# Chunked linear attention and a squared-ReLU layer: a fourth pair of blocks in the paired path, single-value scalars, a folded column sum, two banks lent, and a new order

## The chip, the cores and the metric

One core of a Trainium2 chip runs the whole kernel. The metric is device time in microseconds (us), the median of several executions. The engines are PE (matrix multiply), DVE (vector), ACT (scalar), POOL (GpSimd) and SP, which in this kernel only issues DMAs.

## The reference, cut to what matters

```python
# q, k, v, alpha: [4 batches, 8 heads, 768 steps, 48]
for t in range(S):
    state = alpha[:, :, t, :, None] * state + k[:, :, t] (x) v[:, :, t]     # 48 x 48 a head
    y[:, :, t] = q[:, :, t] @ state
x = y as [3072 tokens, 384]
h = x @ w_in                      # 384 x 2048
g = s * relu(h) ** 2 + b          # s and b are one number each
out = g @ w_out                   # 2048 x 384
```

Since b is one number, `b * (column sums of w_out)` is a row that is added to every row of the output; the kernel works it out once (`bias_w`) and multiplies by s at the very end.

## The kernel before, in words

The 3072 tokens are 24 blocks of 128, six to a batch. For a block the kernel takes logarithms of alpha (`ln2`), sums them along time by a matmul with a triangle of ones (`cum2` or `cumA`), exponentiates both ways (`eb`, `ei`, and `el` for the block's end), scales q and k (`mul1`, `mul2`), transposes them, forms the masked 128 x 128 scores (`A`, `mk`), the state's increment (`KV`, then `t1` on DVE and `sn` on POOL) and the output (`y`, copied out by `ye`). The layer then takes blocks two at a time, as 12 groups: `mm1.g.u.w` is one eighth of a group's first matmul into bank `h_ps[w]`, `re` on ACT is the ReLU into one of two buffers, `sq` on DVE the square, `mm2.n.jq` a quarter of block n's second matmul, `oe` the end on DVE, `st` the store.

Blocks come in two layouts. The first `NPAIR` pairs of blocks are loaded a pair at a time (`ld2`, 384 KB: each partition holds an even and an odd time step, so that each contiguous run in memory is 2 x 48 x 4 = 384 bytes), and use `cum2`, `mul2`, `KV2`, `A2`, `mk2`, `y2`. The later blocks are loaded singly (`ld1`, 192 KB in runs of 192 bytes) and use the forms with a 1; only alpha is always loaded by pairs. Pairs 0 to 2 are transposed on PE (`T2`) and copied out (`Tc2`); from block 6 on `T1` transposes by a DMA from one on-chip buffer to another, issued by SP. Each of q, k, v and alpha has four pair-sized input buffers, so a load waits until the pair four before it has been read.

The weights come in eight blocks of 768 KB: `ld_i.0` to `ld_i.3` for w_in and `ld_o.0` to `ld_o.3` for w_out, into staging buffers. `ci` and `co` cast them to bf16, `cp` adds the two halves of a w_out block, `ca` adds two of these partial sums; `bm` multiplies a tile of ones by b, `bmm` sums over the partitions on PE in fp32, `bc` copies the result out, and the first `oe` waits for it. `ld_bs` loads b and s. `F.n` are n filler matmuls on zeros.

No scheduler runs: the order of everything is the list `PROGRAM`, written out by hand item by item. Each engine, and SP as the queue of DMAs, executes its own items in the list's order, and an item that waits holds all behind it on the same engine. Names carry block, pair or group numbers, and the engine where there is a choice.

Of the kernel before, what the change touches and what calls it, by code (L numbers as in the profile page):

```python
# [8 lines left out]
FP32 = mybir.dt.float32  # L9
# [6 lines left out]
NPAIR = 3  # L16
# [21 lines left out]
ye.1.ACT c_V2 ci.0.ACT ld2.q.2 F.5.h1 KV2.1 mk2.1.1.0 mm1.0.3.1 t1.2 ld2.k.2 mk2.1.0 re.0.3.1.0.ACT
mm1.0.1.0 sn.2.POOL ln2.2 mm1.0.0.1 t1.3 re.0.1.0.1.ACT sq.0.3.0.DVE F.3.o1 y2.1 ci.2.ACT ld_o.2
sq.0.1.1.DVE sn.3.POOL mm1.0.2.0 vc2.2.0.POOL ld1.v.6 re.0.0.1.0.ACT ye.2.DVE vc2.2.1.POOL ye.3.DVE  # L40
cum2.2.1 re.0.2.0.1.ACT sq.0.0.0.DVE ld_o.0 cum2.2.0 eb2.2.1 blk2.2 sq.0.2.1.DVE mm1.1.0.1 ei2.2.1
mul2.q.2.1.DVE eb2.2.0 mm1.1.2.0 ld_i.3 mul2.k.2.1.DVE ei2.2.0 mul2.q.2.0.DVE el2.2 re.1.0.1.0.ACT
mul2.k.2.0.DVE T2.2.0.c re.1.2.0.1.ACT sq.1.0.0.DVE T2.2.1.y Tc2.2.0.c.ACT mm1.1.1.1 ld_o.1 cp.2.DVE
mm1.0.4.0 re.1.1.1.0.ACT Tc2.2.1.y.DVE ld2.a.3 vc1.6.POOL sq.1.2.1.DVE A2.2.0.a sq.1.1.0.DVE mm1.1.3.1
re.0.4.0.1.ACT mk2.2.0 co.2.ACT KV2.2 mm1.0.5.0 co.0.POOL ld1.k.6 t1.4 A2.2.1.a re.1.3.1.0.ACT
sq.0.4.1.DVE mm2.0.0 sn.4.POOL mk2.2.1 re.0.5.0.1.ACT ld1.k.7 mm1.1.4.1 ci.3.ACT ld_bs sq.0.5.1.DVE y2.2
sq.1.3.0.DVE cp.0.DVE re.1.4.1.1.ACT mm1.1.5.0 co.1.DVE ye.5.ACT ye.4.ACT ld1.q.6 cp.1.DVE mm1.2.6.1
ln2.3 ld1.q.7 sq.1.4.1.DVE re.1.5.0.0.ACT cumA.3 ca.0.1.DVE ld_o.3 re.2.6.1.1.ACT blk2.3 mm1.0.6.0 ei1.6
sq.2.6.1.DVE ld1.v.7 sq.1.5.0.DVE eb1.6 mm1.2.4.1 bm re.0.6.0.1.ACT mul1.k.6.DVE mm2.0.1 re.2.4.1.0.ACT
mul1.q.6.DVE mm1.2.3.0 ei1.7 sq.2.4.0.DVE T1.6 eb1.7 sq.0.6.1.DVE mm1.0.7.1 re.2.3.0.0.ACT mul1.k.7.DVE  # L50
KV1.6 mul1.q.7.DVE mm1.2.5.0 re.0.7.1.1.ACT sq.2.3.0.DVE T1.7 el2.3 mm1.2.0.1 sq.0.7.1.DVE
re.2.5.0.0.ACT cp.3.DVE mm1.1.7.0 re.2.0.1.1.ACT ld2.a.4 co.3.ACT mm1.2.1.1 ld1.k.9 sq.2.5.0.DVE
ca.2.3.DVE ld1.k.8 mm2.0.2 ld1.q.8 re.2.1.1.0.ACT t1.6 vc1.7.POOL mm2.0.3 ca.0.2.POOL KV1.7 A1.6 t1.7
mm1.1.6.1 mk1.6 bmm Ay.7 bc ln2.4 ld1.v.9 oe.0 mm2.1.0 ye.6.ACT sq.2.1.0.DVE ld1.q.9 mm2.1.1
sq.2.0.1.DVE re.1.6.1.0.ACT mk1.7 cumA.4 ld2.a.5 blk2.4 mm1.2.7.1 ei1.8 eb1.8 ld1.v.8 mm2.1.2
mul1.k.8.DVE ei1.9 mul1.q.8.DVE mm2.1.3 eb1.9 mul1.k.9.DVE re.1.7.0.1.ACT T1.8 mm2.2.0 vc1.9.POOL oe.1
el2.4 sn.7.POOL mm1.2.2.0 st.0 mm2.2.1 sq.1.7.1.DVE mul1.q.9.DVE mm2.3.0 ln2.5 sq.1.6.0.DVE T1.9 mm2.2.2
re.2.7.1.1.ACT vc1.8.POOL mm2.3.1 st.1 KV1.8 mm2.2.3 t1.8 ld1.v.11 mm2.3.2 ld1.q.10 oe.2 sn.8.POOL Ay.8
ld1.k.11 sq.2.7.1.DVE ld1.k.10 mm2.4.0 ye.7.ACT mk1.8 re.2.2.0.0.ACT KV1.9 mm2.3.3 sq.2.2.0.DVE
mm1.3.3.1 t1.9 mm1.3.7.0 re.3.3.1.1.ACT sn.9.POOL ld1.q.11 Ay.9 mm1.3.6.1 ld1.v.13 ye.8.ACT mk1.9  # L60
re.3.7.0.0.ACT cumA.5 ld1.v.10 blk2.5 oe.3 mm1.3.1.0 eb1.10 el2.5 ld2.a.6 mm2.4.1 eb1.11 mul1.q.10.DVE
ei1.10 mm2.4.2 ei1.11 mul1.k.10.DVE mm2.5.0 sq.3.3.1.DVE T1.10 sq.3.7.0.DVE re.3.1.0.1.ACT mm2.4.3
mul1.k.11.DVE re.3.6.1.0.ACT mul1.q.11.DVE mm2.5.1 sq.3.6.0.DVE T1.11 mm1.3.0.0 vc1.10.POOL vc1.11.POOL
mm2.5.2 re.3.0.0.0.ACT ld1.v.12 KV1.10 ln2.6 mm1.3.2.1 sq.3.0.0.DVE ld1.q.12 oe.4 mm1.3.5.0 st.2
re.3.2.1.0.ACT t1.10 mm2.5.3 st.4 sq.3.1.1.DVE Ay.10 ld1.q.13 ld1.k.12 mm2.6.0 ye.9.ACT mk1.10
vc1.13.POOL re.3.5.0.1.ACT mm1.4.0.1 sq.3.2.0.DVE mm1.4.1.0 ld1.k.13 sq.3.5.1.DVE re.4.0.1.0.ACT
vc1.12.POOL Ay.11 re.4.1.0.1.ACT sn.10.POOL ld1.k.15 mm1.3.4.1 ye.10.ACT oe.5 cumA.6 sq.4.0.0.DVE blk2.6
sq.4.1.1.DVE mm1.4.7.0 ei1.12 ld2.a.8 re.3.4.1.0.ACT mm2.7.0 st.3 el2.6 eb1.12 sq.3.4.0.DVE mm2.7.1
re.4.7.0.1.ACT mul1.q.12.DVE mm2.6.1 mul1.k.12.DVE mm1.4.3.1 mk1.11 T1.12 mm2.6.2 re.4.3.1.0.ACT mm2.7.2
eb1.13 ld2.a.7 ei1.13 mul1.q.13.DVE mm2.7.3 sq.4.7.1.DVE mm1.4.6.0 oe.7 KV1.12 mul1.k.13.DVE mm1.4.2.1  # L70
re.4.6.0.1.ACT T1.13 mm2.6.3 sq.4.6.1.DVE sq.4.3.0.DVE re.4.2.1.1.ACT mm1.4.4.0 t1.12 ld1.k.14 mm1.4.5.1
oe.6 re.4.4.0.0.ACT ld1.v.16 Ay.12 ln2.8 ld1.q.14 ld1.q.15 mm2.8.0 ye.11.ACT mk1.12 ln2.7 mm2.9.0
sq.4.2.1.DVE KV1.13 mm1.5.6.0 t1.13 mm2.9.1 re.5.6.0.1.ACT sn.13.POOL Ay.13 ld1.v.15 sq.5.6.1.DVE
# [24 lines left out]
sq.8.3.1.DVE mk1.19 mm2.14.2 re.8.1.0.1.ACT mm2.15.2 eb1.21 sq.8.1.1.DVE mm1.8.5.1 mul1.k.21.DVE
# [23 lines left out]
def kernel(  # L122
# [130 lines left out]
    def c_ones(*_):  # L253
        nc.gpsimd.memset(ones_f, 1.0)
# [542 lines left out]
```

## Time and profile before

| | |
|---|---|
| time, 3 runs | median 188.2 us (187.43 to 188.76) |
| the profiled execution | 189.13 us, of which the span of the profile is 187.4 us |
| TensorE clock granted | 1.00 |
| busy share of the span | PE 93%, DVE 69%, ACT 57%, POOL 22% |
| DMA | 104586 packets, 34.97 MB; queue q1 77.7% of 16 engines |
| TensorE's last matmul ends | 183.9 us |

The span begins with the first instruction and ends with the last. A line such as L728 is the line of the kernel; SPq is the DMA queue of SP, and "DMA x<-y" a transfer in flight. Blocks are known in the trace by their times: `bmm` is L352, `bc` L361, `cp` and `ca` L338, `oe` L737, the scaling of k and q by pairs L422 and singly L561, `sq` L723, `mm1` L694 and `mm2` L728.

### The profile page before, as it was taken

How to read it: one execution, taken by the hardware profiler on the slowest of the kernel's cores; microseconds unless marked ns; L12 is line 12 of the kernel's file. 1: busy time of each engine (PE TensorE's matmuls, PEld its weight loads, DVE VectorE, ACT ScalarE, POOL GpSimd, SP SyncE). 2: the span in 40 equal slices, each digit the busy share in tenths (PEclk: the TensorE clock that was granted, in tenths of full speed). 3: DMA queues.
4: the chain of work that ended last, by engine and by line, in shares of the span. 5: the costliest groups of instructions: out<-in, count | busy, mean ns of one | idle time of the engine just before them, and what ended most of it. 6: DMA issues, size and time to landing. Idle time of an engine off the chain costs nothing.

```text
span 187.4 us, 5561 instructions
## 1 busy us (share of the span) xinstructions
PE 174.6 (93%) x2297; PEld 124.0 (66%) x2297; DVE 129.5 (69%) x253; ACT 106.9 (57%) x203; POOL 40.6 (22%) x78
## 2 busy tenths in 40 slices
PE   7696997888999999997999999999999999999992
PEld 6474775666566667765667677677677676777761
DVE  2475979979796776449778978588677596364341
ACT  3939996978252565654574565764762643564220
POOL 7198505101343103200111502021201301010000
PEclk9999999999999999999999999999999999999999
DMA  5999999979998799969978999989948554002013
GB/s 149 319 346 372 297 298 382 248 154 262 206 212 177 157 205 178 201 129 249 193 157 207 184 247 172 230 136 240 196 104 166 145 118 123 0 22 110 3 42 126
DMA packets 104586, 34.97 MB, mean 187 GB/s; under 512 B 97905, under 2 KB 103025, under 8 KB 104561
## 3 DMA queue, kind: packets, MB, share of 16 engines
q1 hardware_dynamic: 104560, 34.61, 77.7%
q8 instruction: 18, 0.29, 0.7%
q14 instruction: 8, 0.06, 0.1%
HBM read 25.17 MB, written 4.72 MB: 159 GB/s over the span
## 4 chain that ended last, share of the span: by engine, by line
PE 65%; SPq 20%; DMA 6%; DVE 4%; issue 2%; ACT 0%; DVEq 0%; ACTq 0%
PE o_ps L728 30%; PE h_ps L694 24%; SPq L285 8%; SPq L278 5%; PE py_ps L626 4%; SPq L301 3%; DMA k_in<-in_k_dram 3%; PE a_ps L604 3%; DMA wst<-in_moe_w_out_dram 3%; SPq L307 2%; PE ct_ps L537 2%; PE py_ps L591 1%; DVE gt L723 1%; PE ct_ps L390 1%; DVE colsum L338 1%
## 5 line engine op out<-in xcount | busy, mean ns | idle before, releaser
L704 ACT ACTIVATE r<-h_ps 128x512 bf16<-128x512 f32 x96 | 56.1, 597 | 44.4 <-PE h_ps L694 28.1
L694 PE MATMUL h_ps<-xd,w_in_bf 128*128 128x256 bf16 x576 | 74.3, 273 | 2.6 <-ACT r L704 2.2
L728 PE MATMUL o_ps<-w_out_bf,gt 128*128 128x384 bf16 x384 | 71.3, 326 | 0.0
L694 PEld LDWEIGHTS <-w_in_bf 128*128 128x128 bf16 x576 | 53.9, 98 | 14.2 <-issue 3.4
L723 DVE TENSOR_TENSOR gt<-r 128x512 bf16<-128x512 bf16 x96 | 41.9, 457 | 18.3 <-ACT r L704 17.7
L728 PEld LDWEIGHTS <-gt 128*128 128x128 bf16 x384 | 36.3, 98 | 20.2 <-issue 0.3
L672 POOL TENSOR_TENSOR s_st<-t,blast 128x384 bf16<-128x384 bf16 x16 | 14.4, 902 | 53.1 <-DVE t L662 33.3
L322 POOL CAST vp<-v_in 128x384 bf16<-128x384 f32 x21 | 11.5, 557 | 63.8 <-DMA v_in<-in_v_dram 60.9
L613 DVE TENSOR_TENSOR am<-a_ps,U 128x1024 bf16<-128x1024 f32 x18 | 22.0, 1220 | 2.5 <-PE a_ps L604 2.2
L737 DVE SCALAR_TENSOR_TENSOR o_sb<-o_ps,s_col,bias_w 128x384 f32<-128x384 f32 x24 | 14.6, 614 | 7.7 <-PE o_ps L728 5.5
L320 ACT ACTIVATE xd<-py_ps 128x384 bf16<-128x384 f32 x20 | 9.8, 490 | 12.5 <-PE py_ps L626 12.5
L561 DVE TENSOR_TENSOR qk<-k_in,binv 128x384 bf16<-128x384 f32 x18 | 10.8, 603 | 6.1 <-ACT binv L551 3.5
L662 DVE TENSOR_TENSOR t<-py_ps,s_st 64x192 bf16<-64x192 f32 x28 | 9.9, 354 | 6.6 <-PE py_ps L591 5.1
L369 ACT ACTIVATE la<-a_in 128x768 bf16<-128x768 f32 x12 | 10.1, 843 | 7.4 <-DMA a_in<-in_alpha_dram 7.3
L561 DVE TENSOR_TENSOR qk<-q_in,b_s 128x384 bf16<-128x384 f32 x18 | 10.6, 589 | 3.3 <-DMA q_in<-in_q_dram 1.9
L604 PEld LDWEIGHTS <-qkT 64*128 64x128 bf16 x144 | 4.1, 94 | 4.7 <-issue 4.7
L626 PE MATMUL py_ps<-am,vp 128*32 128x128 bf16 x288 | 7.2, 219 | 0.0
L604 PE MATMUL a_ps<-qkT 64*128 64x128 bf16 x144 | 7.2, 219 | 0.0
L759 PEld LDWEIGHTS <-zeros 128*128 128x128 bf16 x81 | 5.9, 117 | 1.4 <-DVE half L220 1.3
L320 ACT ACTIVATE w_in_bf<-wst 128x1536 bf16<-128x1536 f32 x4 | 5.9, 1482 | 0.2 <-DMA wst<-in_moe_w_in_dram 0.2
L759 PE MATMUL a_ps<-zeros 128*128 128x120 bf16 x48 | 4.4, 273 | 1.3 <-DVE half L220 1.3
L390 PEld LDWEIGHTS <-la 128*128 128x128 bf16 x96 | 3.5, 96 | 3.1 <-issue 2.5
(102 smaller groups left out, 149.9 us busy)
## 6 DMA issues: line engine op xcount, KB each, us to landing
a_in<-in_alpha_dram SPq DMA_DIRECT2D x12, 384.0 KB, 4.6
v_in<-in_v_dram SPq DMA_DIRECT2D x18, 192.0 KB, 4.3
k_in<-in_k_dram SPq DMA_DIRECT2D x18, 192.0 KB, 4.4
q_in<-in_q_dram SPq DMA_DIRECT2D x18, 192.0 KB, 4.2
out_dram<-o_sb SPq DMA_DIRECT2D x18, 192.0 KB, 2.7
wst<-in_moe_w_in_dram SPq DMA_DIRECT2D x4, 768.0 KB, 8.0
wst<-in_moe_w_out_dram SPq DMA_DIRECT2D x2, 768.0 KB, 6.0
gt<-in_moe_w_out_dram SPq DMA_DIRECT2D x2, 768.0 KB, 8.2
```

The lines of the kernel that those rows point to most:

```text
L285: nc.sync.dma_start(out=whole(ins[x], m).rearrange("a s e -> a (s e)").rearrange("a (h f) -> a h f", h=H), in_=src[x][b, :, c * C : (c + 2 ...
L320: nc.scalar.activation(out=out, in_=in_, func=AF.Copy)
L561: on(eng).tensor_tensor(out=half_of(qk, n)[:, "qk".index(x), :, 0:D], in0=half_of(ins[x], n).rearrange("a (h d) -> a h d", d=D), in1=half_ ...
L604: nc.tensor.matmul(out=a_ps[:, e, 128 * p : 128 * p + 128], lhsT=T[r, 1, p, :], rhs=T[r, 0, p, :], start=True, stop=True,)
L613: nc.vector.tensor_tensor(out=half_of(am, n).rearrange("a e p t -> a (e p) t"), in0=a_ps.rearrange("a e (p t) -> a (e p) t", t=128), in1=U ...
L626: nc.tensor.matmul(out=y_out(py_ps, x), lhsT=(st[:, p, c0 : c0 + 32] if e is None else v1[:, p, c0 + 48 * e : c0 + 48 * e + 32]), rhs=qT[: ...
L672: on(eng).tensor_tensor(out=s_sb[n % 3], in0=t1_sb[n % 2], in1=bl.unsqueeze(2).to_broadcast([128, NP, 96]), op=ALU.mult,)
L694: nc.tensor.matmul(out=h_ps[w][:, i * n : (i + 1) * n], lhsT=w_in_bf[:, kk, 128 * j : 128 * (j + 1)], rhs=xd_sb[g % 3][:, kk, 0:n], start= ...
L704: nc.scalar.activation(out=r_sb[i], in_=h_ps[w], func=AF.Relu)
L723: on(eng).tensor_tensor(out=unit_out(g, u), in0=r, in1=r, op=ALU.mult)
L728: nc.tensor.matmul(out=o_ps[n % 2][:, 0:d_model], lhsT=gt_of(n)[:, j, c0 : c0 + C], rhs=w_out_bf[:, j, :], start=(j == 0), stop=(j == NJ - 1),
L737: nc.vector.scalar_tensor_tensor(out=out_sb[n % 3], in0=o_ps[n % 2][:, 0:d_model], scalar=s_col, in1=bias_w, op0=ALU.mult, op1=ALU.add,)
```

## The change

`NPAIR` is 4, so blocks 6 and 7 take the paired path; their transposes stay with the DMA. `KV2` and `t1` of pair 0 use the two `h_ps` banks. b and s are loaded as two single numbers into row 0 of a zeroed tile, spread to all partitions by a matmul with ones (`bsm`) and copied out (`bsc`). `cf` adds the two halves of the summed column tile on DVE, and `bmm` is one matmul in place of two. The order is new throughout, and some items change engine.

```diff
-NPAIR = 3
+NPAIR = 4
 CUM_IN_H = [1]
+KV_IN_H = [0]
...
+    bs_in = sb.tile([128, 2], FP32, name="bs_in")
+    bs = sb.tile([128, 2], FP32, name="bs")
+    b_col, s_col = bs[:, 0:1], bs[:, 1:2]
...
     def c_ones(*_):
         nc.gpsimd.memset(ones_f, 1.0)
+        nc.gpsimd.memset(bs_in, 0.0)
...
     def ld_bs(*_):
-        nc.sync.dma_start(out=b_col, in_=moe_b.to_broadcast((128, 1)))
-        nc.sync.dma_start(out=s_col, in_=moe_s.to_broadcast((128, 1)))
+        nc.sync.dma_start(out=bs_in[0:1, 0:1], in_=moe_b.unsqueeze(0))
+        nc.sync.dma_start(out=bs_in[0:1, 1:2], in_=moe_s.unsqueeze(0))
...
+    def bsm(*_):
+        nc.tensor.matmul(out=o_ps[1][:, 0:2], lhsT=ones_f, rhs=bs_in, start=True, stop=True)
+
+    def bsc(*_):
+        nc.vector.tensor_copy(out=bs, in_=o_ps[1][:, 0:2])
+
+    def cf(eng="POOL"):
+        c = colsum[0]
+        add_on(eng, c[:, 0:d_model], c[:, 0:d_model], c[:, d_model : 2 * d_model])
+
     def bmm(*_):
-        for e in range(2):
-            nc.tensor.matmul(
-                out=o_ps[1][:, 0:d_model],
-                lhsT=bones,
-                rhs=colsum[0][:, d_model * e : d_model * (e + 1)],
-                start=(e == 0),
-                stop=(e == 1),
-            )
+        nc.tensor.matmul(
+            out=o_ps[1][:, 0:d_model], lhsT=bones, rhs=colsum[0][:, 0:d_model], start=True, stop=True
+        )
...
+    def kv_ps(m):
+        return h_ps if m in KV_IN_H else (py_ps, ct_ps)
```

`KV2` writes to `kv_ps(m)[c]`, and `t1` reads `kv_ps(m)[c]` for the paired blocks.

SP's list up to the loads of block 9, before and after (items of SP alone, in their order):

```
before: ld2.a.0 ld2.a.1 ld2.q.0 ld2.k.0 ld2.k.1 ld2.v.0 ld2.q.1 ld2.v.1 ld_i.1 ld_i.0 ld2.a.2 ld_i.2 ld2.v.2
        ld2.q.2 ld2.k.2 ld_o.2 ld1.v.6 ld_o.0 ld_i.3 ld_o.1 ld2.a.3 ld1.k.6 ld1.k.7 ld_bs ld1.q.6 ld1.q.7
        ld_o.3 ld1.v.7 T1.6 T1.7 ld2.a.4 ld1.k.9 ld1.k.8 ld1.q.8 ld1.v.9 ld1.q.9 ...
after:  ld2.a.0 ld2.a.1 ld2.q.0 ld2.k.0 ld2.v.0 ld2.k.1 ld2.q.1 ld_i.1 ld2.v.1 ld_i.0 ld2.a.2 ld_o.0 ld_bs
        ld2.q.2 ld2.k.2 ld2.v.2 ld_o.1 ld_i.3 ld2.v.3 ld_i.2 ld_o.3 ld2.a.3 ld_o.2 ld2.k.3 ld2.q.3 ld2.a.7
        ld2.a.4 ld2.a.6 ld1.q.12 T1.6 T1.7 ld1.v.8 ld1.q.8 ld1.k.9 ld1.k.8 ld1.v.10 ld1.q.9 ld1.v.9 ...
```

Behind the last load of blocks 6 and 7, up to and with the load of block 12's k, SP's list holds T1.6, T1.7 and: before, 3 pair loads, 17 single loads, 4 transposes and the stores of 4 blocks; after, 4 pair loads, 18 single loads, 4 transposes and the stores of 3 blocks. Shortly ahead of that load stand st.2 and st.4 before, T1.10 and T1.11 after.

DVE's list from the end of `t1.3` to the copy of `bias_w`, the same way:

```
before: sq.0.3.0 sq.0.1.1 ye.2 ye.3 sq.0.0.0 sq.0.2.1 mul2.q.2.1 mul2.k.2.1 mul2.q.2.0 mul2.k.2.0 sq.1.0.0 cp.2
        Tc2.2.1 sq.1.2.1 sq.1.1.0 mk2.2.0 t1.4 sq.0.4.1 mk2.2.1 sq.0.5.1 sq.1.3.0 cp.0 co.1 cp.1 sq.1.4.1
        ca.0.1 sq.2.6.1 sq.1.5.0 bm mul1.k.6 mul1.q.6 sq.2.4.0 sq.0.6.1 mul1.k.7 mul1.q.7 sq.2.3.0 sq.0.7.1
        cp.3 sq.2.5.0 ca.2.3 t1.6 t1.7 mk1.6 bc
after:  sq.0.1.1 co.0 sq.0.2.1 cp.0 sq.0.3.0 mul2.q.2.1 mul2.k.2.1 mul2.q.2.0 mul2.k.2.0 sq.1.0.0 sq.0.0.1 bsc
        Tc2.2.0 sq.1.1.0 cp.1 sq.1.3.1 bm mk2.2.0 t1.4 sq.1.2.0 mk2.2.1 co.1 sq.0.6.0 sq.0.7.1 cp.3 sq.1.7.0
        sq.1.6.1 co.3 sq.0.4.0 sq.1.5.1 co.2 cp.2 sq.2.3.1 sq.0.5.0 mul2.k.3.0 mul2.q.3.0 mul2.k.3.1 mul2.q.3.1
        sq.2.5.0 ca.2.3 sq.1.4.0 ca.0.2 sq.2.7.0 cf t1.6 bc
```

Items that change engine: `ci.1` from ACT to POOL; `co.0` from POOL, `co.2` and `co.3` from ACT to DVE; `ca.0.1` from DVE to POOL, `ca.0.2` from POOL to DVE; the scaling of k of pair 1 from POOL to DVE; `ye.2` and `ye.3` from DVE to ACT; the casts of v of pair 2 from POOL to ACT and one of pair 1 the other way; `Tc2.1.1` from ACT to DVE. Fillers are 100 instead of 81.

## The prediction

> **What bounds the kernel now.** I read the page first (slices, then the chain that ended last), then busy time in stretches, then DVE's instructions in order of time, and last DVE's waits.
>
> ```profile
> PE   7696997888999999997999999999999999999992
> DVE  2475979979796776449778978588677596364341
> DMA  5999999979998799969978999989948554002013
> ...
> PE 65%; SPq 20%; DMA 6%; DVE 4%; issue 2%; ACT 0%; DVEq 0%; ACTq 0%
> ```
>
> A slice is 4.7 us. From slice 11 on PE is full but for one dip (slice 19, 84 to 89 us), and the chain is PE's for 65% of the span. Ahead of that it is SP's and the DMAs' (26%). So three stretches: a front of 50 us, PE's own stretch to 183.9, and a tail of 3.5 us (a copy and a store) that the change leaves as it is. In the front, the stretches show two engines at their limit (the columns: busy us of PE, PEld, DVE, ACT, POOL, clock, DMA share, GB/s):
>
> ```profile
> 10.00:15.00 5.00, 4.04 (x104) 3.41 (x108) 4.16 (x8) 1.94 (x6) 4.71 (x9) 1.00 1.11 359
> 20.00:50.00 30.00, 26.73 (x424) 19.41 (x424) 26.31 (x50) 23.41 (x40) 8.01 (x9) 1.00 0.98 266
> 50.00:90.00 40.00, 38.90 (x479) 26.25 (x476) 28.48 (x54) 20.55 (x43) 6.95 (x10) 1.00 0.94 185
> ```
>
> The DMAs are full throughout, and DVE is busy 26.3 of 30 us between 20 and 50. What DVE waits for there and in the dip:
>
> ```profile
> 28.17 0.96 DVE L338 TENSOR_TENSOR colsum<-wst 128x768 f32<-128x768 f32 x1 [1.16 <-DMA wst<-in_moe_w_out_dram]
> 40.98 0.56 DVE L561 TENSOR_TENSOR qk<-q_in,b_s 128x384 bf16<-128x384 f32 x1 [1.20 <-DMA q_in<-in_q_dram]
> 43.99 0.96 DVE L338 TENSOR_TENSOR colsum<-wst 128x768 f32<-128x768 f32 x1 [0.17 <-DMA wst<-in_moe_w_out_dram]
> 49.99 0.56 DVE L361 COPY bias_w<-o_ps 128x384 f32<-128x384 f32 x1 [0.44 <-PE o_ps L352]
> 83.44 0.56 DVE L561 TENSOR_TENSOR qk<-k_in,binv 128x384 bf16<-128x384 f32 x1 [2.65 <-DMA k_in<-in_k_dram]
> ```
>
> The first three are late transfers, and 43.99 is the landing of the last weight block. The dip is one late load, block 12's k. I use `bmm` (L352) as the marker at which both kernels' rests are compared, since the first `oe` and all of the second matmuls behind it need it.
>
> **DMA.** At 10 to 15 us mostly pair loads and weights run, at 359 GB/s: 384 KB take 393,216 B / 359 = 1.1 us, a weight block 2.2. At 50 to 90 single loads dominate: 185 / 0.94 = 197 GB/s, so 192 KB take 1.0 us. A second row for it: alpha of pair 3 landed at 36.41 (the cast that waited for it) and block 6's q at 40.98; between them lie three single loads and the two broadcasts of b and s, 4.57 us. With 1.0 to 1.2 a single load, the broadcasts cost 1.57 to 0.97. Six single loads less, three pair loads more and no broadcasts save 6x - 3.3 + (4.57 - 3x) = 1.27 + 3x, which is 4.3 to 4.9; I take 4.6. Two single numbers I take as nothing: no row shows so small a load, but 0.0 to the 0.5 us that SP needs for any load is its bound. The Trainium skill, "DMA: Bandwidth & Descriptors", section Specifications, asks for at least 512 bytes a piece for line rate, which neither 192 nor 384 reaches; by it three pairs would cost 6.6 and the gain on loads be nil, 1.3 in all. The rows above disagree with that reading, and I go by them.
>
> What comes when: `ld_o.0` stands where `ld_i.2` stood, which landed at 21.64. Alpha of pair 3 has 14 pair loads and 7 weights up to it instead of 13, 1 single load and 7: again 36.4. Then `ld_o.2`, the last weight, 38.6 (before 43.99), and k and q of pair 3 at 39.7 and 40.8.
>
> **DVE up to the marker.** Steps from start to start in DVE's list: `sq` 0.335 (two in 0.67), `cp`, `ca`, `co` 0.87, scalings 0.48, `mk` 1.20, `t1` 0.77, `Tc2` 0.60, `ye` 0.47, `bm` 0.20. Before, from 21.60 to `bc` at 49.99: 18 x 0.335 + 7 x 0.87 + 8 x 0.48 + 3 x 1.20 + 3 x 0.77 + 0.60 + 2 x 0.47 + 0.20 = 23.6 of 28.4 us, so 4.8 of waits: 2.53 for DMAs (the lines above), 0.44 for `bmm`, 0.44 for a `KV` and 1.4 in small pieces. After, up to the end of `cf`: 19 x 0.335 + 10 x 0.87 + 8 x 0.48 + 2 x 1.20 + 0.77 + 0.60 + 0.20, half a `ca` for `cf` (0.45) and 0.2 for the two-column `bsc` (between 0.06, the shortest memset, and 0.56) = 23.5. So DVE does the same work: three casts of w_out and `cf` come, two `ye`, one `mk` and two `t1` fall behind the marker or off it. The casts that ACT and POOL lose were 1.48 each; ACT's ReLUs there stood waiting for DVE, so that saves nothing.
>
> The waits are what changes. `co.2` is DVE's turn after 16.0 us of work, at 37.6, and waits to 38.6: 1.0. `sq.0.4` needs `ld_i.2`, which moved back: 13 pairs and 6 weights, so 3.3 before alpha's 36.4, 33.1; cast 1.48, six matmuls 0.66, ReLU 0.6 give 35.9, and its turn is 36.9: no wait. The other DMA waits go; the small pieces (1.4) stay. That is 21.6 + 23.5 + 2.4 = 47.5, and `bmm` with half its matmuls ends 0.68 later (two of the four that filled 1.35) at 48.2, where before it ended at 49.95: **1.75 us earlier**. Both ends: no waits, 45.8; all of 4.4 as before, 50.2.
>
> Starts ahead of 21.6 I hold equal: the mask comes later on POOL (it follows `vc2.0.0`, up to 0.7), v of pair 1 comes one weight block later (2.2), `ci.1` leaves ACT (1.49) and the lent banks take `KV2.0` off `y2.0`'s banks; I let these cancel and keep 0.7 either way. The 19 more fillers (0.055 each, 1.0) stand where PE waits for a cast or DVE; without that cover they would cost their 1.0.
>
> On POOL, `ca.0.1` (1.80) now runs beside DVE's casts and squares. The trace has such a meeting, at the other end of the front:
>
> ```profile
> 54.23 1.13 POOL L672 TENSOR_TENSOR s_st<-t,blast 128x384 bf16<-128x384 bf16 x1
> 54.59 1.18 DVE L561 TENSOR_TENSOR qk<-k_in,binv 128x384 bf16<-128x384 f32 x1
> ```
>
> where both took longer than alone (0.83 and 0.55). So 0 to 1.8 us may fall on DVE; `ca.0.2` (1.80, from 46.54) ran before beside a `t1` and an `mk` that kept their length (0.74 and 1.23), and the same kind, which reads a PSUM bank, is DVE's next when `ca.0.1` comes; I take 0. The Trainium skill, "SBUF — State Buffer", section SBUF: two separate sides, calls this an exclusive lock between POOL and a DVE instruction with two such inputs; by it the whole 1.8 could count, and the sum would be 187.5.
>
> **PE behind the marker.** Blocks 6 and 7 have 1.46 left (two `A2` of 0.27, `y2.3` 0.75 + 0.17) where 1.17 was left (A 0.33, y 0.34 and 0.50): 0.3 lost. The other work is the same pieces: 1.45 us kept.
>
> **The dip.** From 83.80 to 88.82 PE got through 4 x 0.655 + 0.17 + 0.65 = 3.4 us of work in 5.2 with the late k: 1.8 lost. Ahead of that load SP's list has a pair load and a single load more and a store less, 2.2 less 0.6 to 1.1, say 1.4. Of the 4.6 saved, 3.2 stay, while the work needs k 1.45 earlier: the wait of 2.65 falls to 0.9, and the dip to a third, **1.0 us** gained with rounding down (0 to 1.8). What may be late next is the same load, now behind T1.10 and T1.11 (1.3 each on SP).
>
> **Sum.** 1.45 + 1.0 = 2.45 us off. The profiled execution took 189.13 with a span of 187.4, the median is 188.2; I take the difference off the median: 185.7. With the ends: `bmm` at 45.8 (3.85 off with the 0.3) and the whole dip give 182.5; `bmm` at 50.2 (0.55 on) and no part of the dip give 188.8.
>
> **Rivals.** 1. *Hidden anyway*: DVE's small waits take up part of what the DMAs give back (2.9 of waits instead of 2.4, `bmm` at 48.7) and the dip stays. For it: between 20 and 50 DVE has only 3.7 us idle to give. Against: 2.5 of that are DMA waits. 49.95 - 0.3 - 48.7 = 0.95 off: 187.2. Chance 0.26.
>
> 2. *Slower: DVE held by casts that are ahead of their weights.* `co.2` stands in front of `cp.2`, pair 3's scalings and 5 squares. If `ld_o.2` lands as late as the last block did (43.99), because SP's earlier items hold it, `bmm` ends at 48.2 + 5.4 = 53.6, with the 0.3 of PE's rest 3.95 worse than before; the delay gives block 12's k its time, so the dip's 1.8 is off: 190.3. With the dip gained, it decides from a start of `co.2` at 41.9 (no gain left) and 43.8 (over 1% slower). For it: four casts on an in-order engine. Against: its staging buffer is free from `ci.0` (19.6 before), and SP's list ahead is 5.4 us shorter. Chance 0.17, with the lock on POOL's side counted in.
>
> 3. *The single numbers don't shorten anything* because SP's issue, 1.83 us, not the transfer, was the price and remains for tiny loads: 0.97 to 1.57 less saved, only the dip suffers, 186.4. Chance 0.07.
>
> **How the numbers follow.** The forecast has 0.50. A difference of 1%, 1.9 us, is about what this measurement can tell from none. The forecast's own range, 183 to 187, is mostly beyond 186.3: 0.44 faster of 0.50; with rival 3 at the edge (0.03) and a part of rival 1 (0.08), faster 0.55, slower 0.15 (rival 2 mostly), same 0.30. The range 182.5 to 189.5 takes in the bounds and half of rival 2.
>
> **What would show it.** `ld_o.2` landing near 38.6, `bmm` near 48, DVE's DMA waits between 20 and 50 falling from 2.5 to about 1, the dip at 84 under 1 us, and q1's share of DMA time some 4.6 us of 187 less. It is wrong if DVE's busy time in the front is the same but `bmm` isn't earlier, or if a new dip behind 50 us costs over 1 us: SP held by `ld2.a.7`, which must wait until `ln2.3` has read its buffer, would show as such.

## The result, and the profile after

The kernel after takes 187.61 us (median of 20 executions, 187.35 to 188.97) where the kernel before took 189.0 beside it: ratio 0.9943, 95% interval 0.9926 to 0.996. By the ratio that is 1.1 us less (the two medians lie 1.4 apart), inside the forecast range, but well short of the 2.45 us that the forecast's sum gave. Unchanged and timed again on two chips, it gave 0.9933 and 0.9954 (below). The profiled execution took 188.27 us with a span of 186.5; that of before 189.13 with 187.4.

The page's slices and chain after (a slice is 4.7 us):

```profile
PE   7778896899999999999999999999999999999992
DVE  2489899999786969678675878486797578554512
DMA  5999999969999679889799989949979023012022
...
PE 75%; SPq 11%; DMA 7%; DVE 2%; ACT 2%; issue 1%
```

PE is full from slice 8 on and the dip of slice 19 is gone. The chain is PE's for 75% instead of 65%, and SP's and the DMAs' for 18% instead of 26%. Busy time in the same stretches (busy us of PE, PEld, DVE, ACT, POOL, clock, DMA share, GB/s):

```profile
10.00:15.00 5.00, 3.72 (x95) 3.01 (x98) 4.43 (x8) 0.88 (x2) 4.41 (x13) 1.00 1.07 344
20.00:50.00 30.00, 27.11 (x444) 21.26 (x443) 28.65 (x53) 21.88 (x42) 5.19 (x6) 1.00 1.02 289
50.00:90.00 40.00, 40.00 (x544) 26.97 (x542) 30.25 (x58) 20.42 (x43) 6.57 (x10) 1.00 0.91 190
```

From 50 to 90 PE has no idle time (38.90 of 40 before). From 20 to 50 DVE is busy for 28.65 us where it was for 26.31: its idle time fell from 3.69 to 1.35, but most of what it gained from waits it spent on longer instructions. DVE's own lines show both (start, us, instruction, and the idle time before it with what ended it):

```profile
21.87 1.27 DVE L325 CAST w_out_bf<-gt 128x1536 bf16<-128x1536 f32 x1 [0.23 <-DMA gt<-in_moe_w_out_dram]
...
30.09 1.83 DVE L351 TENSOR_SCALAR bones<-ones_f,bs 128x128 f32<-128x128 f32 x1
35.32 1.22 DVE L325 CAST w_out_bf<-gt 128x1536 bf16<-128x1536 f32 x1
...
40.21 0.95 DVE L325 CAST w_out_bf<-wst 128x1536 bf16<-128x1536 f32 x1
...
48.80 0.56 DVE L369 COPY bias_w<-o_ps 128x384 f32<-128x384 f32 x1 [0.38 <-PE o_ps L364]
```

The DMA waits of this stretch were 1.16 + 1.20 + 0.17 = 2.53 and are 0.23. The last cast (`co.2`, 40.21) waits for nothing, nor do pair 3's scalings at 42.62. But `bm`, which took 0.28 at 39.03 before, takes 1.83 at 30.09, and the casts at 21.87 and 35.32 take 1.27 and 1.22 where an undisturbed one takes 0.95. Together 2.14 us more. What runs beside `bm` is on POOL, and what waits behind it is on PE:

```profile
29.92 1.92 POOL L341 TENSOR_TENSOR colsum<-colsum,colsum 128x768 f32<-128x768 f32 x1 [7.60 <-DVE colsum L341]
```

```profile
33.11 0.42 PE L479 MATMUL a_ps<-qkT 64*64 64x128 bf16 x16 [1.86 <-DVE am L492]
33.46 2.77 PE L705 MATMUL h_ps<-xd,w_in_bf 128*128 128x256 bf16 x22
```

POOL's `ca.0.1` ends at 31.84 and DVE's `bm`, which started after it, at 31.92. The mask behind `bm` is late, and PE stands for 1.86 us.

**The sum in the profiles.** The marker is the start of PE's first matmul behind `bmm`: 49.88 before, where the prediction took the end of `bmm` itself, 49.95. PE's end is the end of its last matmul, the rest lies between them. "Lost in waits" is what the matmuls in the dips took beyond the same pieces elsewhere, and "undisturbed" is the rest without it. The second and third columns are the kernel before run again and with one load moved (`b1_k12_early`); the last two are the kernel after run again (`after_again`, `after_third`).

| us | before | again | k moved | after | again | third |
|---|---|---|---|---|---|---|
| marker | 49.88 | 50.44 | 50.56 | 48.60 | 48.22 | 48.50 |
| PE's end | 183.88 | 184.55 | 183.14 | 182.91 | 182.22 | 182.56 |
| rest | 134.00 | 134.11 | 132.58 | 134.31 | 134.00 | 134.06 |
| lost in waits | 1.42 | 1.63 | 0 | 0.66 | 0.35 | 0.42 |
| undisturbed | 132.58 | 132.48 | 132.58 | 133.65 | 133.65 | 133.64 |

So the marker comes 1.3 to 2.2 us earlier, the waits behind it fall by about 1, and the work behind it takes 1.07 us more. The last row repeats within 0.1 us in each kernel and is the firmest number of this case. Five profiles below that keep the order of the kernel after behind the marker and have no wait of PE there (the first of 2, and 3, 7, 8 and 9) have a rest of 133.74 or 133.75; by them, with nothing taken off, it is 1.16 more than the 132.58 with the load moved.

### The profile page after: what moved, and what is told of

It reads as the page before. It is cut to its first block, busy times and chain, and to the rows that moved or that the text cites. A ratio compares the mean times of both kernels' runs of the same rounds, so it can differ in the third digit from the quotient of the medians.

```text
span 186.5 us, 5704 instructions
## 1 busy us (share of the span) xinstructions
PE 175.3 (94%) x2372; PEld 125.9 (67%) x2372; DVE 133.8 (72%) x260; ACT 102.3 (55%) x201; POOL 38.0 (20%) x76
## 4 chain that ended last, share of the span: by engine, by line
PE 75%; SPq 11%; DMA 7%; DVE 2%; ACT 2%; issue 1%
PE o_ps L739 32%; PE h_ps L705 29%; SPq L288 7%; PE py_ps L637 4%; DMA gt<-in_moe_w_out_dram 4%; DMA qkT<-qk 3%; PE a_ps L615 3%; SPq L310 2%; PE ct_ps L548 2%; SPq L304 1%; ACT r L715 1%; PE py_ps L602 1%; DVE bones L351 1%; PE ct_ps L398 1%; ACT w_in_bf L323 1%
## 5 line engine op out<-in xcount | busy, mean ns | idle before, releaser
L739 PE MATMUL o_ps<-w_out_bf,gt 128*128 128x384 bf16 x384 | 72.4, 326 | 0.2 <-DVE gt L734 0.2
L739 PEld LDWEIGHTS <-gt 128*128 128x128 bf16 x384 | 35.4, 98 | 20.8 <-issue 1.4
L624 DVE TENSOR_TENSOR am<-a_ps,U 128x1024 bf16<-128x1024 f32 x16 | 19.6, 1222 | 8.0 <-PE a_ps L615 7.9
L323 ACT ACTIVATE xd<-py_ps 128x384 bf16<-128x384 f32 x20 | 9.8, 491 | 23.5 <-PE py_ps L637 22.8
L748 DVE SCALAR_TENSOR_TENSOR o_sb<-o_ps,bs,bias_w 128x384 f32<-128x384 f32 x24 | 14.8, 615 | 5.6 <-PE o_ps L739 5.1
L325 POOL CAST vp<-v_in 128x384 bf16<-128x384 f32 x20 | 10.5, 534 | 33.1 <-DMA v_in<-in_v_dram 24.1
L572 DVE TENSOR_TENSOR qk<-k_in,binv 128x384 bf16<-128x384 f32 x16 | 9.1, 575 | 1.3 <-ACT binv L562 1.2
L572 DVE TENSOR_TENSOR qk<-q_in,b_s 128x384 bf16<-128x384 f32 x16 | 8.8, 553 | 1.4 <-ACT b_s L558 0.9
L492 DVE TENSOR_TENSOR am<-a_ps,mask 128x1024 bf16<-128x1024 f32 x6 | 7.3, 1221 | 1.7 <-PE a_ps L479 1.6
L770 PEld LDWEIGHTS <-zeros 128*128 128x128 bf16 x100 | 7.2, 115 | 1.6 <-DVE zeros L213 1.3
L770 PE MATMUL a_ps<-zeros 128*128 128x120 bf16 x72 | 6.2, 259 | 1.3 <-DVE zeros L213 1.3
L430 DVE TENSOR_TENSOR qk<-q_in,b_s 128x384 bf16<-128x384 f32 x6 | 3.2, 551 | 4.5 <-ACT b_s L407 4.4
```

Source lines behind the costliest of these rows:

```text
L572: on(eng).tensor_tensor(out=half_of(qk, n)[:, "qk".index(x), :, 0:D], in0=half_of(ins[x], n).rearrange("a (h d) -> a h d", d=D), in1=half_ ...
L624: nc.vector.tensor_tensor(out=half_of(am, n).rearrange("a e p t -> a (e p) t"), in0=a_ps.rearrange("a e (p t) -> a (e p) t", t=128), in1=U ...
L739: nc.tensor.matmul(out=o_ps[n % 2][:, 0:d_model], lhsT=gt_of(n)[:, j, c0 : c0 + C], rhs=w_out_bf[:, j, :], start=(j == 0), stop=(j == NJ - 1),
L748: nc.vector.scalar_tensor_tensor(out=out_sb[n % 3], in0=o_ps[n % 2][:, 0:d_model], scalar=s_col, in1=bias_w, op0=ALU.mult, op1=ALU.add,)
L770: nc.tensor.matmul(out=bank[to][:, 0:120], lhsT=zeros[:, 0:128], rhs=zeros[:, 0:120], start=True, stop=True)
```

## The experiments

Each was timed in five rounds beside the kernel before on the same chip, and every ratio is to that, with its 95% interval. Edits are to the kernel after unless said otherwise. Runs 1, 5, 8 and the first of 2 shared one chip, 3, 4, 7 and the broadcasts of 6 another, the rest a third. No version was shown to beat the kernel after. The 19 more fillers and the other items that change engine were not run alone.

**1. The kernel after again.** No edit.

> The changed kernel itself, as the yardstick for the runs beside it: 0.994 of the time before (0.9926 to 0.996 measured), the copy of bias_w near 48.8 us of the span and the step that multiplies ones by b (L351) near 1.8 us long, since it starts while POOL adds two partial column sums.

0.9933 (0.9906 to 0.9959), marker 48.22. The gain holds, at 1.1 to 1.3 us.

**2. `bm` ahead of POOL's addition**, twice.

```diff
-... re.1.1.1.0.ACT bsc Tc2.2.0.c.DVE ... ci.3.ACT bm ca.0.1.POOL mk2.2.0
+... re.1.1.1.0.ACT bsc bm Tc2.2.0.c.DVE ... ci.3.ACT ca.0.1.POOL mk2.2.0
```

> The changed kernel with one item moved: DVE multiplies the tile of ones by b right behind the copy of the two scalars, some 2 us before POOL's addition of column sums starts. Theory (the front ends when DVE is through its list, and POOL's addition held DVE for 1.55 us): the step takes 0.28, the copy of bias_w comes 1.2 to 1.5 earlier (47.3 to 47.6 against 48.8), TensorE's last matmul as much earlier, time 0.986 to 0.988 of before. Rival (the front ends by something else, the landing of weights or ACT's ReLUs): the step is 0.28 but the copy of bias_w moves by under 0.5, time 0.992 to 0.994.

> The kernel after with the scaling of the ones by b right behind bsc, once more, on another chip. Theory: the lock between POOL and DVE is avoided and the marker stands at 47.8 to 48.1, 0.4 to 0.6 ahead of the kernel after; ratio to the kernel before 0.988 to 0.993. Rival: the first result was chance, and the ratio is the one of the kernel after, 0.993 to 0.996.

0.9906 (0.9877 to 0.9935) beside 0.9933 of run 1, and on the third chip 0.9953 (0.9918 to 0.9989), where the kernel after, timed later, has 0.9954. The trace of the first one, in order of time:

```profile
28.54 0.29 DVE L351 TENSOR_SCALAR bones<-ones_f,bs 128x128 f32<-128x128 f32 x1
...
30.71 1.93 POOL L341 TENSOR_TENSOR colsum<-colsum,colsum 128x768 f32<-128x768 f32 x1 [7.94 <-DVE colsum L341]
...
32.16 0.42 PE L479 MATMUL a_ps<-qkT 64*64 64x128 bf16 x16 [0.24 <-DVE am L492]
```

`bm` is back at 0.29 and PE's wait falls from 1.86 to 0.24, so the meeting with POOL is what made it long. But the marker came only to 47.84, 0.4 to 0.8 earlier than in the three profiles of after, and to 49.68 in the second profile, where DVE's first cast (`co.0`) waited 0.9 for its weights and the scaling of pair 3's q 0.4. PE's stall of 1.9 us was not on the path that sets the marker in full. A gain in time over the kernel after is not shown: the intervals overlap on the first chip, and the second time there was none.

**3. The same with v of pair 2 cast later on ACT** (`e7_bm_v`), to see what stands behind the lock.

```diff
-... vc2.2.0.ACT mul2.q.2.0.DVE el2.2 re.1.0.0.0.ACT mul2.k.2.0.DVE
+... mul2.q.2.0.DVE el2.2 re.1.0.0.0.ACT vc2.2.0.ACT mul2.k.2.0.DVE
```

> The changed kernel with the ones-times-b step behind the scalars' copy as in the run with that alone, and with ACT's cast of the first v of pair 2 behind the next ReLU, so that a late v no longer holds the exponential that pair 2's transposes wait for. Theory (the lock's 1.55 us sits on the chain mask, scores, mm1 of group 0): second scores of pair 2 at 31.3 to 31.6 instead of 33.1, copy of bias_w at 47.0 to 47.6, time 0.986 to 0.989 of before. Rival (the front has a second limit close behind): 0.990 to 0.992.

0.9949 (0.9919 to 0.9979), marker 48.17. Two pieces of the chain that ended last (start, us, what):

```profile
34.48 8.09 DMA q_in<-in_q_dram
...
42.66 1.49 DVE qk L430 x3
```

The marker now follows the landing of pair 3's q at 42.57. The prediction had it at 40.8. So a second limit stood close behind the lock: the marker is 0.1 to 0.4 us earlier than in the three profiles of after, which differ by as much among themselves.

**4. Loads earlier and POOL's addition on DVE as well** (`e8_bm_v_order`): on top of 3, `ld_i.3` and `ld_o.1` change places, `cp.1` goes behind `mk2.2.1`, and `ca.0.1` runs on DVE.

```diff
-... ld_o.1 ... ld_i.3 ... cp.1.DVE ... ca.0.1.POOL mk2.2.0 ... mk2.2.1 ...          ca.2.3.DVE
+... ld_i.3 ... ld_o.1 ...                          mk2.2.0 ... mk2.2.1 cp.1.DVE ... ca.0.1.DVE ca.2.3.DVE
```

> As the run before, and the fourth block of w_in is loaded ahead of the second of w_out; that one's column sum moves behind pair 2's masks and the addition of the two sums from POOL to DVE. Theory (once the lock is gone, that block of w_in, landing at 30.8, holds group 0's last units): mm1 of group 0 goes on at 31.1 to 31.5, DVE has 0.87 more, copy of bias_w 46.4 to 47.4, time 0.983 to 0.988 of before. Rival (DVE's list is full, and its 0.87 more comes on top): copy of bias_w 47.6 to 48.4, 0.990 to 0.993.

1.0002 (0.997 to 1.0033), marker 48.88. Busy time from 20 to 50:

```profile
20.00:50.00 30.00, 27.07 (x440) 20.71 (x439) 28.24 (x53) 22.09 (x41) 3.30 (x5) 1.00 1.06 289
```

Without POOL's addition DVE is still busy for 28.24 of 30 us. From the landing of a block of w_out, at 36.48, to the end of `cf` at 48.09 the chain that ended last is DVE's but for 0.6 us. So the third limit is DVE's list itself, and the 0.87 us that `ca.0.1` takes there come on top. The time shows no gain over the kernel before.

**5. Three pairs in the new order** (`e2_three_pairs`): `NPAIR` is 3, and blocks 6 and 7 take the single path at the same places of the order.

```diff
-NPAIR = 4
+NPAIR = 3
...
-ld2.v.3 ... ld2.k.3 ... ld2.q.3 ... mul2.k.3.0 mul2.q.3.0 ... KV2.3 ... A2.3.0.a ... y2.3
+ld1.v.6 ld1.v.7 ... ld1.k.6 ld1.k.7 ... ld1.q.6 ld1.q.7 ... mul1.k.6 mul1.q.6 ... KV1.6 ... KV1.7 A1.6 ... y1.7
```

> The changed kernel without the fourth pair: NPAIR is 3, blocks 6 and 7 load, scale, score and end singly (six single loads for three pair loads), each item in the place of its paired twin. Theory A (the pair's loads save 3.3 us of DMA time in the front, and that is worth more than its matmuls cost): DMA waits of DVE before the marker return by 1 to 2.5, behind the marker TensorE has 0.6 to 1.0 less work, time 0.997 to 1.002 of before. Theory B (the DMAs have slack there since the weights now come first, so the pair only adds matmuls): no new waits, time 0.988 to 0.991.

0.9983 (0.9955 to 1.0011), marker 49.54. Part of DVE's waits for DMAs is back, 0.74 us, less than the 1 to 2.5 of theory A:

```profile
37.65 0.96 DVE L341 TENSOR_TENSOR colsum<-wst 128x768 f32<-128x768 f32 x1 [0.46 <-DMA wst<-in_moe_w_out_dram]
44.03 0.56 DVE L572 TENSOR_TENSOR qk<-q_in,b_s 128x384 bf16<-128x384 f32 x1 [0.28 <-DMA q_in<-in_q_dram]
```

The fourth pair is worth 0.9 to 1.3 us at the marker, nearly as much as the whole gain in time (the intervals of this run and of run 1 just overlap). Queue q1 was busy for 78.8% of 187.1 us here, 147.4 us, and for 142.9 to 144.7 in the three profiles of after; the prediction's price for the pair's loads, 6x - 3.3 or 2.7 to 3.9 us, is in line with that. The Trainium skill, "DMA: Bandwidth & Descriptors", Specifications, wants at least 512 bytes a piece for line rate; read as no gain between 192 and 384 bytes, it does not fit this run.

**6. Broadcasts again** (`e3_broadcast`), and the other way round the single numbers in the kernel before (`b2_single_values`).

```diff
-        nc.sync.dma_start(out=bs_in[0:1, 0:1], in_=moe_b.unsqueeze(0))
-        nc.sync.dma_start(out=bs_in[0:1, 1:2], in_=moe_s.unsqueeze(0))
+        nc.sync.dma_start(out=bs[:, 0:1], in_=moe_b.to_broadcast((128, 1)))
+        nc.sync.dma_start(out=bs[:, 1:2], in_=moe_s.to_broadcast((128, 1)))
...
-... bsm ... bsc ...
```

> The changed kernel with b and s loaded by broadcast to 128 partitions again, at the place of the single numbers in SP's list, and without the matmul and the copy that spread them. Theory (each broadcast costs SP and the DMAs something like the 1.0 to 1.6 us together that the forecast took): loads behind it 1.0 to 1.6 later, the copy of bias_w 0.3 to 1.2 later than beside it (48.4 to 48.8), time 0.996 to 1.000 of before. Rival (DVE and TensorE, not the loads, set the front by now): the loads are later but the copy of bias_w is not, time 0.992 to 0.994.

> The kernel before with one part of the change alone: b and s loaded as two single numbers, spread by a matmul and copied out, at the place in SP's list where the broadcasts stood. Theory: SP's 1.83 us for the broadcasts falls to some 0.6, block 6's q lands about 1 us earlier, DVE's wait of 1.20 for it goes, but the last weight block stays a limit and the marker, which waits for POOL's addition behind DVE's, moves 0.3 to 1.0 earlier; ratio 0.995 to 0.999. Rival: the loads behind are bound by the DMAs and not by SP's issue, so q lands where it did and the two new instructions cost 0.2: ratio 1.0 to 1.001.

With broadcasts 0.9973 (0.9941 to 1.0004), marker 48.18; single numbers in the kernel before 0.9963 (0.9928 to 0.9998), marker 50.21. SP's issue of the two, first in the kernel before run again, then with single numbers:

```profile
35.67 1.08 SPq L313 DMA_DIRECT2D b_col<-in_moe_b_dram  x1
36.80 0.79 SPq L314 DMA_DIRECT2D s_col<-in_moe_s_dram  x1
```

```profile
35.30 0.43 SPq L315 DMA_DIRECT2D bs_in<-in_moe_b_dram  x1
35.78 0.23 SPq L316 DMA_DIRECT2D bs_in<-in_moe_s_dram  x1
```

SP is free 1.2 us earlier, and in `b2_single_values` block 6's q came without a wait; but the last weight block then let DVE wait 1.52 at 44.27, and the marker did not come earlier than in the first profile of before. With the broadcasts back in the kernel after, DVE waits for no load between 20 and 50, and the marker is where it was. Both ratios point to a gain of 0.2 to 0.4%. It is not settled: one interval ends at 0.9998, just short of none, and the other holds the 0.9943 of the kernel after.

**7. `KV2` and `t1` of pair 0 in the banks of before** (`e5_kv_own_banks`), with a filler between them taken from another bank.

```diff
-KV_IN_H = [0]
+KV_IN_H = []
...
-F.6.y
+F.6.h0
```

> The changed kernel with k^T v of pair 0 in the banks that y uses (and six fillers in another bank, since theirs is now taken). Theory (the lent banks take a wait off pair 0's y): its y waits for the second t1, 1.0 to 1.5 us later, and a third to all of it reaches the copy of bias_w; time 0.995 to 1.001 of before. Rival (the first weights and v of pair 1 hold the next step anyway): time 0.992 to 0.994.

0.9961 (0.9932 to 0.9989), marker 48.40: PE waits 0.85 for POOL at 18 us, and nothing of it reaches the marker. This part is worth nothing that can be seen.

**8. Two casts on ACT** (`e6_casts_act`).

```diff
-... ye.4.ACT mm1.1.5.0 ... co.3.DVE ... mm1.2.3.0 co.2.DVE ... el2.3
+... ye.4.ACT co.3.ACT mm1.1.5.0 ...     mm1.2.3.0 ...          el2.3 co.2.ACT
```

> The changed kernel with the casts of the last two blocks of w_out (the third and the fourth) on ACT again, 1.48 each, instead of DVE, 0.87 each. Theory (DVE's list sets the end of the front): DVE saves 1.74, the copy of bias_w comes 1.0 to 1.7 earlier, time 0.985 to 0.989 of before. Rival (ACT, busy 22 of 30 us there, passes its 2.96 on through the ReLUs to the squares): no gain or a loss, time 0.994 to 1.0, DVE's waits for ReLUs in the front up by 1 to 2.

1.0083 (1.0046 to 1.0119), marker 53.12. DVE then waits for ACT:

```profile
42.62 0.91 DVE L734 TENSOR_TENSOR gt<-r 128x512 bf16<-128x512 bf16 x2 [2.43 <-ACT r L715]
...
48.96 0.43 DVE L734 TENSOR_TENSOR gt<-r 128x512 bf16<-128x512 bf16 x1 [1.39 <-ACT r L715]
```

The casts on DVE are worth 1.5% in this order: the theory missed, and the loss is larger than the rival had it. The prediction said that what ACT loses "saves nothing", since its ReLUs waited for DVE. Here the squares wait for the ReLUs, 4.9 us in all. The marker is later than this alone makes it: the profile is of the slowest of the ten executions (192.53, the median is 190.69), and the granted clock was 0.66 from 35 to 40, some 1.7 us of PE's work.

**9. `bmm` as two matmuls, no `cf`** (`e4_two_bmm`).

```diff
-    def bmm(*_): one matmul, rhs=colsum[0][:, 0:d_model]
+    def bmm(*_): two matmuls, e in 0, 1, rhs=colsum[0][:, d_model * e : d_model * (e + 1)]
...
-cf.DVE
```

> The kernel after without the fold: cf is gone and the sum over partitions is two matmuls of PE again. Theory: DVE loses 0.48 us of work ahead of the marker, PE gains two fp32 passes, 0.65 to 0.7, so the marker comes 0.2 later, within what can be told: ratio to the kernel before 0.994 to 0.997. Rival: DVE's list is the limit and the two matmuls fill time in which PE waits, so the marker comes 0.3 to 0.5 earlier: ratio 0.991 to 0.993.

0.9995 (0.9959 to 1.0031), marker 50.85. This profile has a stretch in which the granted clock was 0.67:

```profile
35.00:40.00 5.00, 5.00 (x109) 3.52 (x108) 4.59 (x8) 3.86 (x7) 1.10 (x3) 0.67 1.12 357
...
45.00:50.00 5.00, 5.00 (x53) 3.82 (x51) 4.59 (x10) 2.68 (x5) 0.00 (x0) 1.00 1.31 231
```

Up to 33.48 PE had stood idle for 2.24 us, behind the same `bm` as in the kernel after (1.83 us again). 0.67 of the clock over 5 us is 1.65 us of work less, which is in this marker. PE was busy all through the last stretch, so the two matmuls (1.30 instead of 0.65) filled no idle time there. The direction is the first theory's; the size is not settled, as the interval holds 0.997.

**10. One load earlier in the kernel before** (`b1_k12_early`, `b1_again`), beside that kernel unchanged (`before_again`) and the kernel after (`after_third`).

```diff
-... ld1.v.12 KV1.10 ln2.6 ... ld1.q.12 oe.4 mm1.3.5.0 st.2 ... st.4 ... ld1.q.13 ld1.k.12
+... ld1.k.12 ld1.v.12 KV1.10 ln2.6 ... ld1.q.12 oe.4 mm1.3.5.0 st.2 ... st.4 ... ld1.q.13
```

> The kernel before, with one item moved: the load of block 12's k goes from behind the stores of blocks 2 and 4 to ahead of the load of block 12's v, five SP items earlier. It tests the term for the dip alone. Theory: the dip at 84 us (1.42 us of idle PE) is the late load and nothing else, so it vanishes, the marker stays at 49.9, TensorE's last matmul ends at 182.5 instead of 183.9, and the time falls by 1.4 us, ratio 0.992 to 0.995: as much as the whole change gives. Rival: PE would have waited anyway, for block 12's v or q or for the exponentials, and the dip keeps at least 0.7; ratio 0.996 to 1.0.

> The kernel before with the load of block 12's k five SP items earlier, once more and beside the kernel before. Theory: no dip, PE's rest behind the marker 132.6 again, and a gain in time that is only what the dip costs in a usual execution, 0.3 to 0.8 us: ratio 0.996 to 0.9985. Rivals: the dip costs its 1.4 in every execution, ratio 0.992 to 0.994; or the load ahead of the stores delays something that the profile of the first one doesn't show, ratio 1.0 to 1.003.

> The kernel before unchanged, for a second profile of it. What it decides: whether the dip of 1.42 us at 84 us and the marker at 49.9 are what every execution has. Theory: the dip and the marker go against each other, since block 12's k comes when SP's list lets it come, so with the marker later by some tenths the dip is smaller by as many, and PE's end is 183.5 to 184.0 in both. Rival: the dip is a fixed 1.4 behind the marker wherever this stands.

> The kernel after unchanged, a third profile beside the two of before. Theory: marker 48.2 to 49.5, rest 133.7 to 134.3, ratio 0.992 to 0.997. Rival: the first results were those of one chip, ratio 0.998 or more.

Load moved: 1.0005 (0.9971 to 1.0039) and 1.0009 (0.9985 to 1.0033). Before again 1.0016 (0.9985 to 1.0047), after again 0.9954 (0.9931 to 0.9976). The stretch from 50 to 90 in the first profile with the load moved:

```profile
50.00:90.00 40.00, 40.00 (x485) 26.81 (x485) 29.59 (x56) 22.16 (x45) 6.81 (x10) 1.00 0.96 192
```

The dip is gone and the rest is 132.58, yet the time is what it was. This profile is of the fastest of its twelve executions (188.39, the median is 189.52), and the other two show more. First two views of the kernel before again (busy time, PE in order of time), then PE and DVE of the second profile with the load moved:

```profile
50.00:90.00 40.00, 38.53 (x470) 25.94 (x472) 28.53 (x55) 20.72 (x43) 7.10 (x10) 1.00 0.95 191
```

```profile
75.54 0.40 PE L604 MATMUL a_ps<-qkT 64*128 64x128 bf16 x8 [1.47 <-DMA qkT<-qk]
```

```profile
74.87 0.40 PE L604 MATMUL a_ps<-qkT 64*128 64x128 bf16 x8 [0.86 <-DMA qkT<-qk]
```

```profile
78.96 0.62 DVE L737 SCALAR_TENSOR_TENSOR o_sb<-o_ps,s_col,bias_w 128x384 f32<-128x384 f32 x1 [1.71 <-DMA out_dram<-o_sb]
```

The unchanged kernel loses 1.63 us in this execution too, but at 74 us, on the transpose of block 10, and nothing at 84. Neither the theory nor the rival for `before_again` had this. So the dip is not one late load: with k early (second profile) PE waits at 74 us all the same, and which item it meets late changes from execution to execution. The profiles fit a stream of SP and the DMAs that is late as a whole between 60 and 90; the `oe` at 78.96 waits 1.71 for a store, and one in the first profile of before 1.9. No run shows directly what makes it late, nor all of why the time stayed the same. The kernel after loses little there in its three profiles; the largest wait of the third:

```profile
102.11 0.40 PE L615 MATMUL a_ps<-qkT 64*128 64x128 bf16 x8 [0.26 <-DMA qkT<-qk]
```

**11. The small sums back beside their `cumA`** (`e9_blk_together`), for blocks 10 and later.

```diff
-... blk2.5 mm2.4.1 ... cumA.5 mm2.5.1
+... mm2.4.1 ...        cumA.5 blk2.5 mm2.5.1
```

> The kernel after with each small sum blk2 of blocks 10 and later put back right behind its cumA, where the kernel before has it, instead of between two of the layer's matmuls. Theory: each change from a small matmul back to one of the layer costs PE 0.03 to 0.08 us, so PE's rest behind the marker falls by 0.2 to 0.4, from 133.7 to between 133.3 and 133.5; the time moves by less than can be told, ratio 0.991 to 0.997. Rival: the rest is longer for the pair's scores and outputs alone, and stays at 133.7.

0.9986 (0.9964 to 1.0007), marker 48.27, rest 134.79. New waits came with it:

```profile
88.80 0.40 PE L615 MATMUL a_ps<-qkT 64*128 64x128 bf16 x8 [0.27 <-DMA qkT<-qk]
...
102.41 0.40 PE L615 MATMUL a_ps<-qkT 64*128 64x128 bf16 x8 [0.28 <-DMA qkT<-qk]
```

The theory missed. The 0.28 us that `mm2` pieces behind a `blk2` had been longer did go, but pieces elsewhere became as much longer, and with the waits taken off (an estimate of 0.9 us from the pieces around them), the rest is about 133.9: no less. What exactly lengthens the matmuls behind a change of work stays open.

## Why the prediction was right and wrong, step by step

The direction held, and so did the mechanism in the main: DVE's waits for loads go, and the marker and the stretch behind it gain. The size did not: the work behind the marker, forecast as 0.3 us longer, is over 1 us longer, and took most of the marker's gain back.

| step | forecast, us | measured in the profiles, us |
|---|---|---|
| marker earlier | -1.75 | -1.28 in the first two profiles, means -1.72 |
| work behind the marker | +0.3 | +1.07, means +1.12 |
| dip | -1.0 | -0.76, means -1.05 |
| sum | -2.45 | -0.97, means -1.65 |

The means are those of the two profiles of before and the three of after. `before_again` ran at 0.97 of full clock from 20 to 50, which is in its marker. In time the difference was 1.1.

**DMA prices: right for the pair, wrong for the broadcasts.** Pair loads cost less than two single ones (5). DVE's DMA waits fell from 2.53 to 0.23, below the 1.0 that the sum had left for `co.2`; but with three pairs in the new order they are 0.74, so most of the fall comes with the rest of the change and not with the pair. The places in time were too early: q of pair 3 was priced at 40.8 and landed at 42.57 in the profile that shows it (3). The 0.97 to 1.57 us for the broadcasts were read between 36.4 and 41.0 of the kernel before, where the DMAs were not full (the last two numbers are their share and GB/s):

```profile
36.40:41.00 4.60, 4.34 (x44) 3.29 (x43) 3.40 (x8) 4.41 (x9) 0.00 (x0) 1.00 0.71 122
```

With the broadcasts back no load is waited for (6): they cost SP time, and no run shows a cost to the DMAs. The sign that q1's time would fall by 4.6 us did not come: by its share of the span it is 145.6 and 143.3 us in the two profiles of before, and 142.9, 144.6 and 144.7 after.

**DVE's list up to the marker: the sum came close by misses that cancel, which is luck.** The forecast had the same work (23.5), 2.4 us of waits and a start at 21.6. The list began at 21.21, the waits nearly went, and `bm` and two casts took 2.14 us more beside POOL. The step that failed here is "I take 0" for POOL's `ca.0.1`, which looked at DVE's next PSUM reader and not at `bm`, which stands directly ahead of `ca.0.1` in the list. The row of before that had both engines longer (54.23 and 54.59) was the nearer one. The Trainium skill, "SBUF — State Buffer", section SBUF: two separate sides, names a DVE instruction in a two-port mode or with two inputs in SBUF, and has whichever starts second, it or POOL's, blocked until the first ends. Here DVE's 1.83 us ended 0.08 us behind POOL's addition, which agrees; `bm` has one tensor input, and no run shows which of the two cases it is. Its 187.5 was the better sum, though not for its reason alone: with the lock taken away (2, 3) the marker gained 0.8 us at most, since pair 3's q (3) and DVE's own list (4) stand close behind it.

**PE behind the marker: the step that cost the forecast its size.** The two terms that failed are "0.3 lost" for blocks 6 and 7 and "the same pieces" for all the rest, which put its change at nothing. Blocks 6 and 7 were to have 1.46 us left instead of 1.17. The trace gives 1.82 instead of 1.22 (0.33, 0.39 and 0.50): scores of a pair take 0.35 each there (33.11 to 33.46 above), not 0.27, and `y2.3` 1.12, not 0.92. By kind, from each start to the next, in profiles without waits behind the marker (the first with the load moved in the kernel before; run 3 of the new order), scores and outputs rose from 14.24 to 14.84, the small sums and `KV` from 7.36 to 7.45, and the layer's matmuls, "the same pieces", from 110.98 to 111.45: in all 1.16 where 0.3 was forecast. The new order changes between small and large matmuls at more places, and the prediction priced no such change. Run 5 tells the two terms apart. With three pairs in the new order the layer's matmuls take 111.48, so their 0.5 us come with the order; the 0.6 of scores and outputs come with the pair. (Its rest is 134.01 all the same: 0.21 of it is a wait, and the scores and the `KV` of one block, 0.33 and 0.27, stand behind the marker there and ahead of it in the kernel before.) Why the order makes the layer's matmuls longer stays open (11).

**The dip: right in size, which is luck, and wrong in its cause.** About 1 us came back. But the prediction read one late load out of one profile, and 10 shows PE waiting with that load early; moving the load alone gained nothing that shows. Its 1.8 us lost also rests on a slip: 83.80 to 88.82 are 5.0 us and not 5.2, so 1.6 by its own figures, and 1.42 in the table.

**Rivals.** The first (187.2, hidden anyway) is nearest to the measured time, though the dip did not stay, as it had it. The second did not happen: `co.2` found its weights in place. Casts that hold an in-order engine did cost 1.5%, but on ACT (8). The third is contradicted in its premise, as SP's issue fell from 1.87 to 0.66 us (6); its outcome, that they shorten nothing that reaches the marker, fits 6 all the same.

## What to carry to other kernels

Compare two orders of work by a marker only after listing, by kind, how long the bound engine works on either side of it: here 1.07 of the 1.3 to 1.7 us gained ahead of it came back as longer work behind. A wait seen in one profile may stand elsewhere in the next: profile the unchanged kernel twice before pricing it, and test it alone. A price for a transfer read from two landings holds only if the DMAs were full between them. And before a POOL instruction is put beside DVE, look at the DVE instruction that starts next to it, not at the typical one.

## What the runs showed of the hardware

A DVE instruction with one tensor operand on chip and a column of scalars (0.28 us alone) took 1.83 us beside POOL's addition, and fp32 to bf16 casts 1.22 to 1.27 instead of 0.95. The granted TensorE clock was 0.67 and 0.66 from 35 to 40 us in the two profiles in which PE had stood idle for 2.24 and 2.30 us up to 33.5 and 33.8 (9, 8), and stayed at 1.00 behind the 1.86 us of the kernel after. But it was also 0.79 from 20 to 25 in `before_again`, where PE had last stood idle for 1.30 us, up to 18.05; so no threshold is shown. From execution to execution of the same kernel the marker moved by 0.4 (three profiles of after), 0.6 (two of before) and 1.8 us (the two of run 2), so one profile's marker does not settle a few tenths. The undisturbed rest of PE repeated within 0.1.
